# A fused linear-attention, Fourier-mixing and MLP kernel whose instruction order is a table: the table is replaced

## The chip, the cores and the metric

The kernel runs on 1 core of one Trainium2 chip. The metric is the device time of one execution in microseconds (us). The core has five engines that run side by side, each through its own list of instructions in order: TensorE (PE, matrix multiplications), VectorE (DVE), ScalarE (ACT), GpSimd (POOL) and SyncE (SP, which here only starts transfers). They wait for each other through semaphores.

## The reference

Inputs are r, k, v of shape (4, 8, 768, 48), w and u of shape (8, 48), and two MLP weights. What is computed, cut to what matters:

```python
for t in range(768):                                   # attention with a decaying state, per batch and head
    cur = einsum('bhd,bhe->bhde', u * k_t, v_t)
    y[:, :, t] = einsum('bhd,bhde->bhe', r_t, state + cur)
    state = w[None, :, :, None] * state + einsum('bhd,bhe->bhde', k_t, v_t)
x = y as (4, 768, 384)
X = fft(fft(x, axis=1), axis=2)                        # Fourier mixing, real part only
h = x + real(X)
hn = (h - mean(h)) / sqrt(var(h) + 1e-6)
out = h + relu(hn @ w_ch1) @ w_ch2                     # 384 -> 1536 -> 384
```

## The kernel before

The 768 steps of each batch are cut into 6 chunks of 128, so there are 24 chunks. Per chunk, k, r and v are loaded (192 KB each). k and r are scaled by powers of w from the tables `wtab` (the instructions with the output KR; one on DVE or POOL for each of k and r, or one on DVE for both), transposed by TensorE and copied out of PSUM (KRT), or transposed by a DMA in later chunks. Then come a score product (PSUM bank), a copy (AC) and a mask (MA) of it on ACT and POOL, or the mask straight on DVE, the u term (PR, DE, TT), the running state (S) and the output X.

A batch whose six chunks are done is folded by symmetry: HH and XF are sums and differences of halves of X, with the tensor XF as the input of the first transform (line 636 on TensorE, tables te_t and tn_t). In batch 0 this is done chunk by chunk, so the XF of its last two chunks (numbers 4 and 5) is the last input that its first transform needs. A second transform (lines 677), the residual and the statistics (UF, UB, st, MV), a transposition of the normalised rows (UNT), the first MLP product (line 765, copied out as HT) and the second (line 786, and 812 for the very last rows, added up as osb) follow for each batch. The results go out by DMA from POOL (line 799) or SP (line 800, and 822 for two half tiles at the end).

The first thing of all is the table wtab: w is loaded (line 283, the first transfer on ScalarE's queue), broadcast over the partitions by a product with a row of ones (line 322; the ones are a memset on DVE, line 286, into a part of the HT buffer), its logarithm is taken (line 324) and six exponentials are made of it (lines 326 and 328), with `icol` and `ncol` (lines 304 and 305, converted on DVE from an iota on POOL, line 288) as their factors.

No compiler orders the work. Every operation is first recorded with a number, what it reads and writes, and a list of alternatives (which engine does it, and how). `ORDER` is a table that gives the numbers in the order in which they are issued; a token such as `173.1` means operation 173 in its alternative 1. `emit` walks over it, gives each new tile the buffer of its ring that was last used longest ago, and calls the chosen alternative:

```python
for k, (n, a) in enumerate(order):
    o = self.ops[n]
    for t in o["new"]:
        ends = held[t.ring]
        m = min(range(len(ends)), key=ends.__getitem__)
...
    fn = o["alts"][a][2]
    if fn is not None:
        fn()
```

Operations 0 to 149 are matrix products of zeros (line 272) that compute nothing and may be left out; some products of zeros of 384 columns (line 366) inside the chunks are optional too. An engine's list is the subsequence of ORDER that falls to it, so the table sets each engine's order, which engine does what where there is a choice, and the buffers.

Of the kernel before, what the change touches and what calls it, by code (L numbers as in the profile page):

```python
# [95 lines left out]
152 15 159 158 28 150 160 46 151 174 155 164 8 165 173.1 196 193 202 32 34 199.1 205 203 153 208 176 181 200.1 154 182  # L96
183 184 185 187 206 209 214 215 204 207 180.1 169.1 166.1 168.1 175.1 170.1 157 178.1 172 167 274.1 156 275.1 278.2
276.1 279.2 186 310.1 211 212 201.1 378.2 189 217 271 179.1 311.1 312.1 316.1 210 280.2 213 161 315.1 281.2 188 347.1
349.1 379.2 162 163 415.3 314.1 317.1 348.1 318.1 282.2 284 351.3 353.3 319.1 283.2 352.3 287 382.1 354.3 195 198
380.2 297 333 190 191 220 218 285.1 320 216 197 221 177 384.1 385.1 321.1 286.1 194 223 301.1 277 302.1 355.3 289  # L100
383.1 386.1 288 226 303.1 337.1 452 219 304 323 313 388 222 224 296.1 453 305.1 272 227 357 322.1 324 291 325 391
306.2 513.2 387 401 339 417.3 356 420.1 389 332.1 416.3 390 358.1 359.1 338.1 350 421.1 225 423.1 6 235 419.1 392
422.1 454 362 481.1 405 360 458 482.1 307 456 459 340.1 341 424 308 364 368.1 438 381 406 342.1 457 460 363 369.1 425
426.1 361 393 428.1 429.1 442.1 427.1 461 514.2 309.1 343 1 400.1 462 465.1 370 371.1 344 346.1 372 345.1 41 418 407
430 463.1 517 443.1 466.1 273 373.1 408.1 409 444 410.1 485.2 1021 467 411.1 437.1 473 445.1 236 446 374.1 483.1 487.2
1014 486.2 488.2 455 447.1 1015 1022 412 414.1 375.1 43 546.3 515.2 464.1 519 471.1 472.1 1007 1008 489.2 491 474.1
494.1 413 377 448 376 475 484 573.2 1023 490 1009 1010 495.1 449.2 1024 450.1 1016 1017 496 476.1 477 478.2 480 479
520 1000 1001 503.1 1309 518 1002 1003 504 508.1 451 1004 1005 547.3 548.3 521 522.1 552.1 492.1 509.1 1006 1025 1026
1018 1019 493.1 510 1011 1012 551.1 1020.1 554.1 516 1013 1028 511 523 524.1 528 512 550.1 228 1027 535.1 1030 553.1
1042 1029 526 536 1058 1059.1 1308 1060.1 1061 574.2 575.2 1064 1065.1 1031 1032 1043 1078 1044 525.1 1070 1036 1037  # L110
549.2 1071 1066.1 577.2 1079.3 1072 556 557.1 579.2 542 580.2 540.1 555.1 1038 1073.2 563 567.1 559.1 1050 1033.2
578.2 1051.4 1052.4 1045.2 1055.4 1067 1081.3 581.2 569 1080.3 1039.2 1053.4 1057.4 1083.3 1085.3 560.1 1084.3 561 232
244 229 230 676.3 562 231 558.1 568.1 233 583 1082.3 586 1062.1 677.3 1371 1373 570 245 1377 234 571 680.3 584 585
639.1 1056.4 678.3 682.3 1375 582.1 1054.4 237 681.3 587 238 239 683.3 1355 572 684.3 1363 1359 1356 1374.1 1372 241
240 1378.1 686 1364 243 596 1365 1369 687 527 688 247 248 171 1360 541.1 640.1 689 690 600 576 601 606.2 608.2 543 544
1376.1 685 1366 1313 1370.1 1314 765.3 1361 588 602 595 1325 545 1074.1 1317 1318.1 1362 1075.1 1333 1334 603 607.2
1034.1 1040.1 604 1321 1331 1315 1335 1332 643.3 1327 605 1336 612.2 1322.1 609.1 641.1 621 1316 628.1 1323 645.3 1324
767.3 611.2 614.2 646.3 644.3 766.3 610.2 647.3 613.2 615 1326 1367 1368 771.4 246 250 251 1357 1310 616 617 1035.1
249 649 648 619.1 620.1 650 1311 708.1 679.2 629 635 1358 1319 1328 654 660 658.1 652.1 653.1 633.1 634.1 242 1329
1330 1320 699 691 703.1 618 636 1391 642.2 659.1 704.1 789.2 637 705 638 661 770.4 651 662 663 1063.1 192 1349 1379  # L120
709.1 769.4 706 707 1068.1 1069.1 1076.1 1343 664 1312 666 710.1 712 1350 1380 698.1 665 667 1337 1392 1344 713 668
1046.1 714 1041.1 1047.1 670 669 671 715 1338 1345 744.2 716 718 721 1351 1339 1346 1048.1 711 1352 1340 672 673 675
674 719 723 1094 1086 1087 741.2 1049 742.2 1353 730.1 1090 1091 1092 1088 756 1347 790.2 791.2 722 793.4 1095 1098
795.4 1096 1099 1100 717 1341 1089 773.4 720 794.4 1393 731 797.4 1394 1093 1097.1 735.1 772.4 775 1101 774 1104 1348
1105 1116 1381 768 1102.2 1103 757 776 1117 1106 813.3 1132 814.3 1110 1382 782 783.1 1118 745.4 815.3 1107 778 1111
1112 780 1125.4 818.4 785 1385 736.1 1119 1129.4 1113 737 738 739 1077 779 1133 784.1 792 1134 1152 1144 1386 1387
781.1 740 1136.1 1137.1 804 1138 1124 805.1 1145 1146 786 777 1135 787 743.2 1139 796.4 798.1 1395 1396 1388 817.4
1140 819.4 820.4 821.4 823 799 1141.2 1126.4 1155.4 746.4 1383 1147 1127.4 1157.4 802.1 806 809 807.1 1108.1 1354
1131.4 822.1 747.4 800.1 1128.4 1130.4 1153.4 1156.4 788 1397 801.1 1399 808.1 252 824 1398 1405 1406 825 1401 749.4
# [752 lines left out]
```

## Time and profile before

| | us |
|---|---|
| median of 3 runs | 179.48 (178.18 to 181.58) |
| profiled execution, its own time | 177.02 |
| its span, first to last instruction | 175.3 |
| TensorE busy in the span | 157.2 |
| VectorE busy | 138.7 |
| ScalarE busy | 108.4 |
| GpSimd busy | 80.8 |

The span is what the profile's times count from; 1.72 us of the profiled time lie outside it. The profiled execution was 2.46 us shorter than the median of the timed runs, and the three timed runs lie 3.4 us apart among themselves.

### The profile page before, as it was taken

To read this page: it belongs to the slowest core of one execution; us is meant where nothing else is said; L and a number is where in the kernel's file an instruction comes from. 1 tells how busy PE (TensorE), PEld (TensorE's weight loads), DVE (VectorE), ACT (ScalarE), POOL (GpSimd) and SP (SyncE) were. 2 spreads that over 40 slices of the span, in tenths; PEclk is the share of its full clock that TensorE was granted. 3 is DMA by queue.
4 is the path that set the end of the run, shared out by engine and by line. 5 is a ranking of instruction groups with operands and counts; after the bars stand their busy time and mean duration, and the time that the engine had idled before them with its cause. 6 is when DMAs were issued, how large, how long until landed. Compare 5 with 4: busy or idle time off the path is not lost. (4 is left out here: it accounts for less than half of the span.)

```text
span 175.3 us, 4260 instructions
## 1 busy us (share of the span) xinstructions
PE 157.2 (90%) x1589; PEld 111.8 (64%) x1590; DVE 138.7 (79%) x314; ACT 108.4 (62%) x260; POOL 80.8 (46%) x120
## 2 busy tenths in 40 slices
PE   6348989829999979999999899999999999999992
PEld 1136667627777756677666478667676876666661
DVE  5487999999988979999979998868899775511632
ACT  2375889528868995578996266957735770275210
POOL 6606947693776640466974453473452121020110
PEclk9999999999999999999999999999999999999999
DMA  5999989799099999999999989999500043420132
GB/s 117 219 202 212 245 166 221 181 186 175 2 184 177 203 212 201 186 238 138 213 199 230 267 174 244 187 138 227 152 0 0 4 121 81 112 95 0 45 124 100
DMA packets 98118, 27.08 MB, mean 155 GB/s; under 512 B 94369, under 2 KB 96930, under 8 KB 98098
## 3 DMA queue, kind: packets, MB, share of 16 engines
q1 hardware_dynamic: 92912, 21.70, 63.2%
q0 software_dynamic: 2064, 4.53, 11.0%
q10 hardware_dynamic: 3122, 0.59, 2.1%
q8 instruction: 12, 0.20, 0.5%
q14 instruction: 8, 0.07, 0.1%
HBM read 19.77 MB, written 4.72 MB: 140 GB/s over the span
## 5 line engine op out<-in xcount | busy, mean ns | idle before, releaser
L765 PE MATMUL bank<-UNT,W 128*128 128x384 bf16 x288 | 54.4, 326 | 0.0
L786 PE MATMUL bank<-W,HT 128*128 128x384 bf16 x276 | 51.9, 326 | 0.9 <-DMA W<-in_moe_w_ch_dram 0.9
L770 ACT ACTIVATE HT<-bank 128x384 bf16<-128x384 f32 x68 | 30.6, 494 | 27.2 <-PE bank L765 27.0
L765 PEld LDWEIGHTS <-W 128*128 128x128 bf16 x288 | 30.6, 114 | 11.5 <-DMA UNT<-UB 0.2
L786 PEld LDWEIGHTS <-HT 128*128 128x128 bf16 x276 | 25.9, 98 | 15.7 <-DMA W<-in_moe_w_ch_dram 1.1
L453 POOL TENSOR_SCALAR_AFFINE_SELECT MA<-AC 128x512 bf16<-128x512 bf16 x25 | 17.3, 701 | 10.8 <-ACT AC L451 8.4
L796 DVE SCALAR_TENSOR_TENSOR osb<-bank,rstd,UF 128x384 f32<-128x384 f32 x23 | 13.9, 614 | 9.3 <-PE bank L786 9.1
L386 POOL TENSOR_TENSOR KR<-kr,wtab 128x384 bf16<-128x384 f32 x15 | 16.5, 1106 | 7.3 <-DMA kr<-in_r_dram 5.4
L771 DVE TENSOR_SCALAR HT<-bank 128x384 bf16<-128x384 f32 x28 | 15.0, 552 | 6.1 <-PE bank L765 6.0
L386 DVE TENSOR_TENSOR KR<-kr,wtab 128x384 bf16<-128x384 f32 x29 | 16.5, 586 | 3.1 <-ACT wtab L326 2.8
L451 ACT CAST AC<-bank 128x512 bf16<-128x512 f32 x25 | 14.2, 586 | 4.1 <-PE bank L444 2.0
L799 POOL DMA_DIRECT2D out_dram<-osb x11 | 6.3, 568 | 22.0 <-DVE osb L796 19.9
L636 PE MATMUL bank<-te_t,XF 128*128 128x193 bf16 x108 | 12.2, 247 | 4.5 <-DVE XF L567 3.8
L456 DVE TENSOR_TENSOR MA<-bank,mtri 128x512 bf16<-128x512 f32 x23 | 15.4, 683 | 0.7 <-PE bank L444 0.6
L708 ACT ACTIVATE tn_t<-UF,sm 128x384 bf16<-128x384 f32 x24 | 14.8, 617 | 0.2
L410 PE MATMUL bank<-ident,KR 128*128 128x128 bf16 x112 | 12.0, 251 | 3.0 <-DVE KR L386 2.8
L432 POOL TENSOR_TENSOR PR<-KRT 128x512 bf16<-128x512 bf16 x9 | 10.4, 1156 | 7.3 <-ACT KRT L420 4.1
L636 PEld LDWEIGHTS <-XF 128*128 128x128 bf16 x120 | 9.9, 97 | 5.7 <-DVE XF L567 4.0
L689 DVE SCALAR_TENSOR_TENSOR UF<-bank,X 128x384 f32<-128x384 f32 x22 | 11.6, 548 | 1.7 <-PE bank L677 1.7
L410 PEld LDWEIGHTS <-KR 128*128 128x128 bf16 x112 | 8.8, 113 | 5.8 <-issue 3.5
L523 DVE TENSOR_TENSOR TT<-V,bank 128x384 bf16<-128x384 bf16 x19 | 10.3, 544 | 2.6 <-PE bank L514 2.5
L543 DVE TENSOR_TENSOR X<-bank,TT 128x384 bf16<-128x384 f32 x18 | 9.6, 550 | 2.4 <-PE bank L535 2.4
(108 smaller groups left out, 263.8 us busy)
## 6 DMA issues: line engine op xcount, KB each, us to landing
kr<-in_k_dram SPq DMA_DIRECT2D x23, 192.0 KB, 4.2
kr<-in_r_dram SPq DMA_DIRECT2D x23, 192.0 KB, 4.4
vt<-in_v_dram SPq DMA_DIRECT2D x23, 192.0 KB, 4.3
out_dram<-osb SPq DMA_DIRECT2D x12, 192.0 KB, 1.9
out_dram<-osb POOLq DMA_DIRECT2D x11, 192.0 KB, 3.1
W<-in_moe_w_ch_dram POOLq DMA_DIRECT2D x2, 576.0 KB, 7.5
W<-in_moe_w_ch_dram POOLq DMA_DIRECT2D x3, 384.0 KB, 6.2
te_t<-te_c SPq DMA_DIRECT2D x1, 579.0 KB, 5.4
```

What stands on the lines that cost most here:

```text
L386: eng.tensor_tensor(out=o, in0=x, in1=y, op=AluOp.mult)
L410: nc.tensor.transpose(tps[s]()[:, p, :], KR()[:, s, p, :], ident)
L451: op(("AC", i, a), [("ACT", "AC", lambda: nc.scalar.copy(AC(), A_ps[a]())), ("NONE", "", None)], r=[("A", i)], w=[("AC", i, a)], new=[AC], ...
L453: op(("MA", i, a), [("POOL", "MA", lambda: nc.gpsimd.affine_select(out=MA[a](), in_=AC(), pattern=[[0, NP], [1, 128]], base=0, channel_mul ...
L456: ("DVE", "MA", lambda: nc.vector.tensor_tensor(out=MA[a](), in0=A_ps[a](), in1=mtri.unsqueeze(1).to_broadcast([128, NP, 128]), op=AluOp.m ...
L636: nc.tensor.matmul(fp()[:, par, :], lhsT=lhsT[:, g * CH:g * CH + 128], rhs=rhs, start=(nb == 0 and par == 0), stop=(nb == last and par == ...
L708: ("ACT", "SQ", lambda: nc.scalar.activation(out=squares, in_=UF()[:, j, :], func=Act.Square, scale=-float(DM), bias=sm()[:, j:j + 1], acc ...
L765: nc.tensor.matmul(hp(), lhsT=W1[:, dt, ft // 4 * 512 + ft % 4:(ft // 4 + 1) * 512:4], rhs=UNT()[:, :, dt, :], start=(dt == 0), stop=(dt = ...
L770: op(("HT", hf, ft), [("ACT", "HT", lambda: nc.scalar.activation(out=HT()[:, ft, :], in_=hp(), func=Act.Relu, scale=-1.0)), ("DVE", "HT", ...
L771: ("DVE", "HT", lambda: nc.vector.tensor_scalar(out=HT()[:, ft, :], in0=hp(), scalar1=-1.0, scalar2=0.0, op0=AluOp.mult, op1=AluOp.max))],
L786: nc.tensor.matmul(mo(), lhsT=HT()[:, ft, j * 128:(j + 1) * 128], rhs=W2[:, ft, :], start=(ft == 0), stop=(ft == 11))
L796: one(("osb", hf, j), "DVE", "osb", lambda: nc.vector.scalar_tensor_tensor(out=osb(), in0=mo(), scalar=rstd()[:, j:j + 1], in1=UF()[:, j, ...
```

## The change

ORDER is another table. No function and no operation's definition changes; every line of code moves up by one, since the new table is one line shorter (line 386 of the profile is line 385 after the change). The diff's first lines stand for the rest:

```diff
-152 15 159 158 28 150 160 46 151 174 155 164 8 165 173.1 196 193 202 32 34 199.1 205 203 153 208 176 181 200.1 154 182
-183 184 185 187 206 209 214 215 204 207 180.1 169.1 166.1 168.1 175.1 170.1 157 178.1 172 167 274.1 156 275.1 278.2
+208 209 202 150 151 203 152 155 204 205 206 158 199.1 159 200.1 207 214 215 211 212 213 30 169 216 210 163 175 181.1
+154 160 201.1 166 167 168 164 165 170 153 182 183 184 185 274.1 275.1 172 174 156 171 178.1 276.1 188 280.1 278.1 162
...
```

Besides the order, some 230 operations change their engine, or are split or merged by their alternative. Over the whole kernel, DVE gets 5 fewer HT copies and ACT 5 more; ACT gets 6 more KRT copies and DVE 6 fewer; POOL starts 15 of the result's transfers in place of 11, and SP 10 in place of 14. The products of zeros of 512 columns go from 10 to 2, those of 384 columns from 1 to 4. Loads keep their size and number.

The start on DVE. KR, WD, XF and S are buffers that are set to zero once; the memset of `HT 1x128` is the row of ones for the first product. Before:

```order
L285 MEMSET zero 128x256
L296 MEMSET wuc 128x4
L295 MEMSET wuc 128x4
L316 MEMSET XF_100 128x6x16
L304 CAST icol<-icol_i 128x3
L305 TENSOR_SCALAR ncol<-icol 128x3
L336 MEMSET WD_82 64x4x48 x2
L286 MEMSET HT_186 1x128
L316 MEMSET XF_101 128x6x16
```

After:

```order
L284 MEMSET zero 128x256
L294 MEMSET wuc 128x4
L295 MEMSET wuc 128x4
L308 MEMSET KR_93 128x16x8
L313 MEMSET WD_83 128x384
L286 MEMSET HT_186 128x128
L308 MEMSET KR_90 128x16x8
L308 MEMSET KR_91 128x16x8
L308 MEMSET KR_92 128x16x8
L303 CAST icol<-icol_i 128x3
L304 TENSOR_SCALAR ncol<-icol 128x3
L308 MEMSET KR_94 128x16x8
L285 MEMSET HT_186 1x128
```

Four memsets of KR, one of WD and one of HT stand ahead of the cast of icol now (all of them were on POOL or stood later on DVE), and one of KR stands between ncol and the row of ones in place of two of WD.

The start on POOL, where wuc are four loads of w and u by columns. Before:

```order
L302 DMA wuc<-in_w_dram 48x4x1
L288 ISA
L288 IOTA icol_i 128x3
L315 MEMSET WD_82 128x384
L320 MEMSET S_97 128x384
L310 MEMSET KR_93 128x16x16
L310 MEMSET KR_90 128x16x16
L310 MEMSET KR_92 128x16x16
L315 MEMSET WD_83 128x384
L310 MEMSET KR_94 128x16x16
L292 AFFINE_SELECT mtri<-HT_186 128x128
```

After:

```order
L287 ISA
L287 IOTA icol_i 128x3
L301 DMA wuc<-in_u_dram 48x4x1
L319 MEMSET S_98 128x384
L301 DMA wuc<-in_w_dram 48x4x1
L288 AFFINE_SELECT ident<-HT_186 128x128
L319 MEMSET S_95 128x384
L301 DMA wuc<-in_u_dram 48x4x1
L301 DMA wuc<-in_w_dram 48x4x1
L385 TENSOR_TENSOR KR_91<-kr_103,wtab_78 128x8x48
```

The iota comes first, and the unbroken row of seven memsets is replaced by memsets and selects between four DMA issues.

The end of batch 0's fold on DVE. The last three XF are those of chunks 4 and 5. Before:

```order
L561 TENSOR_TENSOR HH0_99<-X0_142,bank2_63 128x192
L558 TENSOR_TENSOR HH0_99<-X0_142 128x192
L561 TENSOR_TENSOR HH0_99<-X0_142,bank4_65 128x192
L567 TENSOR_TENSOR XF0_100<-HH0_99 128x196
L567 TENSOR_TENSOR XF0_100<-HH0_99 128x2x98
L567 TENSOR_TENSOR XF0_100<-HH0_99 128x196
L386 TENSOR_TENSOR KR0_90<-kr2_104,wtab2_79 128x8x48
```

After:

```order
L560 TENSOR_TENSOR HH0_99<-X0_142,bank1_62 128x192
L455 TENSOR_TENSOR MA1_131<-bank4_65,mtri_70 128x512
L557 TENSOR_TENSOR HH0_99<-X0_142 128x192
L385 TENSOR_TENSOR KR1_91<-kr1_103,wtab1_78 128x8x48
L431 TENSOR_TENSOR PR3_126<-KRT3_122 128x512
L560 TENSOR_TENSOR HH0_99<-X0_142,bank3_64 128x192
L566 TENSOR_TENSOR XF0_100<-HH0_99 128x2x98
L566 TENSOR_TENSOR XF0_100<-HH0_99 128x196
L566 TENSOR_TENSOR XF0_100<-HH0_99 128x2x98
L385 TENSOR_TENSOR KR0_90<-kr0_102,wtab2_79 128x8x48
```

A mask, a KR and a PR of later chunks stand among the last HH now, ahead of the three XF.

The same place on POOL; the two DMA of W1 load the first MLP weight. Before:

```order
L567 TENSOR_TENSOR XF0_100<-HH0_99 128x2x98
L840 DMA W1_88<-in_moe_w_ch1_dram 128x3x768
L386 TENSOR_TENSOR KR0_90<-kr2_104,wtab2_79 128x8x48
L432 TENSOR_TENSOR PR3_126<-KRT3_122 128x512
L840 DMA W1_88<-in_moe_w_ch1_dram 128x3x768
L386 TENSOR_TENSOR KR2_92<-kr3_105,wtab0_77 128x8x48
L403 CAST V3_117<-vt1_109 128x384
```

After:

```order
L566 TENSOR_TENSOR XF0_100<-HH0_99 128x196
L839 DMA W1_88<-in_moe_w_ch1_dram 128x3x768
L402 CAST V1_115<-vt5_113 128x384
L839 DMA W1_88<-in_moe_w_ch1_dram 128x3x768
L385 TENSOR_TENSOR KR0_90<-kr0_102,wtab2_79 128x8x48
L452 AFFINE_SELECT MA3_133<-AC1_128 128x512
L431 TENSOR_TENSOR PR0_123<-KRT1_120 128x512
```

Between the two issues of W1 stands one cast, where a KR and a PR stood; KR, a select and PR follow.

The last transfers on SP, results (osb) and transposes of UB. Before:

```order
L747 DMA_TRANSPOSE UNT_154<-UB_179 128x9x128
L800 DMA out_dram<-osb_189 128x384 x2
L800 DMA out_dram<-osb_187 128x384
L822 DMA out_dram<-osb_190 128x192
L822 DMA out_dram<-osb_188 128x192
```

After:

```order
L746 DMA_TRANSPOSE UNT_152<-UB_180 128x9x128
L799 DMA out_dram<-osb_190 128x384
L799 DMA out_dram<-osb_188 128x384
L799 DMA out_dram<-osb_190 128x384
L821 DMA out_dram<-osb_188 128x192
```

The second half tile is gone from SP: `L821 DMA out_dram<-osb_189 128x192` is now the last row of POOL, and the last of all to be issued.

## Rows read from the trace of the kernel before

**Rows 1.** The page, part 1: busy us, share and instructions by engine.

```profile
PE 157.2 (90%) x1589; PEld 111.8 (64%) x1590; DVE 138.7 (79%) x314; ACT 108.4 (62%) x260; POOL 80.8 (46%) x120
```

**Rows 2.** Busy time by stretches: stretch, its length, engines, granted clock, DMA share, GB/s.

```profile
9.10:20.00 10.90, 8.04 (x90) 6.29 (x90) 9.38 (x23) 7.74 (x18) 5.13 (x6) 1.00 1.27 230
20.00:40.00 20.00, 14.91 (x220) 11.94 (x218) 19.80 (x41) 13.17 (x31) 14.22 (x20) 1.00 0.97 187
40.00:110.00 70.00, 68.06 (x742) 49.49 (x741) 64.56 (x148) 52.27 (x129) 38.55 (x52) 1.00 0.96 190
110.00:172.00 62.00, 61.78 (x538) 42.83 (x535) 40.10 (x91) 32.15 (x82) 16.78 (x24) 1.00 0.39 91
```

**Rows 3.** What TensorE waited for: us in total, times, longest.

```profile
PE bank L636 <- DVE XF L567: 3.8, 2, 3.1
...
PE bank L786 <- DMA W<-in_moe_w_ch_dram: 0.9, 1, 0.9
```

**Rows 4.** The timeline, start of the program: start, length, engine, what, idle before it.

```profile
1.85 0.60 ACTq L356 DMA_DIRECT2D kr<-in_r_dram  x1
...
2.45 0.44 POOL L315 MEMSET WD<- 128x384 bf16 x1
...
2.56 2.07 DVE L304 CAST icol<-icol_i 128x3 f32<-128x3 int32 x1 [1.23 <-POOL icol_i L288]
...
4.28 0.32 POOL L310 MEMSET KR<- 128x256 bf16 x1
...
5.41 0.17 DVE L286 MEMSET HT<- 1x128 f32 x1
...
5.63 1.64 PE L322 MATMUL bank<-HT 1*128 1x384 f32 x2 [1.62 <-DVE HT L286]
...
7.31 0.49 ACT L324 ACTIVATE HT<-bank 128x384 f32<-128x384 f32 x1 [4.66 <-PE bank L322]
```

**Rows 5.** DMA issues on the page: KB each, median us from issue to landing.

```profile
kr<-in_r_dram ACTq DMA_DIRECT2D x1, 192.0 KB, 5.0
...
out_dram<-osb SPq DMA_DIRECT2D x2, 96.0 KB, 1.6
```

**Rows 6.** DVE's groups from 8.4 to 38.2 us: busy, mean ns, idle before.

```profile
L386 DVE TENSOR_TENSOR KR<-kr,wtab 128x384 bf16<-128x384 f32 x12 | 7.2, 624 | 2.9 <-ACT wtab L326 2.8
...
L456 DVE TENSOR_TENSOR MA<-bank,mtri 128x512 bf16<-128x512 f32 x8 | 5.4, 682 | 0.0
L421 DVE COPY KRT<-bank 128x512 bf16<-128x512 bf16 x7 | 2.8, 416 | 0.8 <-PE bank L410 0.8
```

**Rows 7.** The timeline around the last XF, DVE, then POOL.

```profile
34.12 3.98 DVE L567 TENSOR_TENSOR XF<-HH 128x196 bf16<-128x196 bf16 x3
...
34.23 0.80 POOL L840 DMA_DIRECT2D W<-in_moe_w_ch_dram  x1
35.05 1.00 POOL L386 TENSOR_TENSOR KR<-kr,wtab 128x384 bf16<-128x384 f32 x1
36.00 1.15 POOL L432 TENSOR_TENSOR PR<-KRT 128x512 bf16<-128x512 bf16 x1
37.09 0.79 POOL L840 DMA_DIRECT2D W<-in_moe_w_ch_dram  x1
```

**Rows 8.** The XF instructions: ns least, median, most; first and last start.

```profile
L567 DVE TENSOR_TENSOR XF<-HH x7: 249/519/3180, 23.7 to 37.5; 128x196 bf16<-128x196 bf16 x7
```

**Rows 9.** TensorE's timeline: four transposes each, either side of 22.4 us.

```profile
21.70 0.63 PE L410 MATMUL bank<-ident,KR 128*128 128x128 bf16 x4 [0.22 <-POOL MA L453]
...
22.45 0.41 PE L410 MATMUL bank<-ident,KR 128*128 128x128 bf16 x4
```

**Rows 10.** The timeline at the end: the last instruction of DVE.

```profile
171.95 0.42 DVE L819 SCALAR_TENSOR_TENSOR osb<-bank,rstd,UF 128x192 f32<-128x192 f32 x1 [0.30 <-PE bank L812]
```

**Rows 11.** POOL's issues of results (line 799): ns, and us to landing.

```profile
L799 POOL DMA_DIRECT2D out_dram<-osb x11: 540/573/592, 75.5 to 168.0; - x11
...
DMA to landing us min/median/max: 2.1/3.1/3.8
```

121 rows, old and new, of the table ORDER are left out of this document.

## The prediction

> **What bounds the kernel now.** I read the page's busy times first, then the busy times by stretches, TensorE's waits, and the timeline at the three places where it waits or where the change moves something. TensorE is busy 157.2 us [rows 1], and the stretches say where it is not [rows 2]: the first 9.1 us are the start, 9.1 to 20 us lack 10.90 - 8.04 = 2.9 us, 20 to 40 us lack 5.1 us, 40 to 110 us lack 1.9 us, 110 to 172 us lack 0.2 us, and from 172 us there is only the last result's way out, 3.3 us. So from 40 us on TensorE is the bound and nearly full, and only some 2 us can be saved there. Before 40 us it is VectorE that is full (19.80 of 20.00 us) and TensorE that waits for it. The largest wait is for XF, 3.8 us in two waits, one of them 3.1 [rows 3].
>
> That wait is not work. Of VectorE's last three XF, which together take 3.98 us, one alone took 3.18, though the least of the seven is 0.249 [rows 7, 8]. In the same time GpSimd ran issue, KR, PR and issue without a gap [rows 7]. VectorE's instruction was held while GpSimd was at work. The start shows the same thing: the cast of icol, 3 columns, took 2.07 us, from 2.56 to 4.63, while GpSimd's memsets ran from 2.45 to 4.28 + 0.32 = 4.60 [rows 4]. Since the ones for the first product stand behind it on VectorE (5.41), the product (5.63), the logarithm (7.31) and all of wtab come late by that.
>
> **The change part by part.** I sum against the profiled execution's own 177.02 us.
>
> The start. VectorE is idle for 1.23 us before the cast, so it was free at 1.33 [rows 4]. In place of one small memset the new list has six ahead of the cast; five at the 0.17 of the ones' memset and WD, the widest, at GpSimd's 0.44 for as many columns give 1.3 us at most [rows 4], less the one left out: the cast is reached at about 2.5. GpSimd stands then at the end of its memset of S or in the DMA issue behind it. The best case is that the cast isn't held at all: 0.17 for each of cast, ncol, one memset and the ones end at 3.2. The worst is that it is held through GpSimd's whole unbroken list, which with two more memsets or selects of 0.44 and three issues of 0.57 to 0.80 [rows 4, 7, 11] from 2.5 on ends at 5.1 to 5.8, and the ones at 5.6 to 6.3 in place of 5.58. I take a value between, nearer the best: the last XF started at 37.5, so the long one ended about there, some 0.4 us into the second issue of W (37.09), and an issue seems to let VectorE in where a run of other work doesn't [rows 7, 8]. That gives 3.0 for the cast and 3.5 for the ones. The product also needs w, whose landing no row shows; the nearest are 1.6 us for half a tile and 5.0 us for r on the same queue [rows 5], so from 2.4 to 5.8 us. I take the product at 4.1 in place of 5.63: **-1.5 us**, bounds -2.4 and +0.7. The loads do not take this back: r of chunk 0, issued at 1.85, lands 5.0 later [rows 4, 5], at 6.9, and the scaling of r comes about 1.5 us after the logarithm, at 7.3. The third load that now stands behind it on ScalarE's queue, v of chunk 0, comes after it. Eight products of zeros that are left out, six of them at the start, cost nothing in time: TensorE has no other work there; what they may do for its clock is a rival.
>
> The chunks of batch 0, from the first KR to the last XF, where VectorE is the bound. VectorE loses two KR, three KRT copies and one mask, 2 x 0.62 + 3 x 0.42 + 0.68 = 3.2 us [rows 6]. It gains six and loses two instructions of the kinds HH, XF, PR, S, X and V, none of them cheaper when free than 0.25 [rows 8] or dearer than the mask's 0.68 [rows 6]: +1.0 to +2.7; and some seven memsets, at most 0.2 each. Together -2.2 to +0.9, and I take 0: the stage is not shorter, it starts earlier. ScalarE and GpSimd, which take what VectorE gives up, have room (13.17 and 14.22 of 20 us) [rows 2], but what GpSimd takes can hold VectorE more often.
>
> The last three XF. Before, GpSimd's issue, KR, PR and issue lasted 3.7 us [rows 7]. Now issue, cast, issue, KR and select stand there: 0.80 + about 0.5 + 0.79 + 1.00 + about 0.6 = 3.7 us, as long. But VectorE meets them with a mask, HH, KR, PR and HH first, some 2 us of work, so part of that list is over when the XF come; on the other hand HH, KR and PR have two inputs in SBUF, as XF has, and can be held as well. From -3.2 (nothing held) to +2.0 (each held in turn); I take **-0.5**. What is late next if the hold goes: the second transform and UF of batch 0, on a VectorE that has 5.4 us free between 40 and 110 [rows 2], so a gain here reaches TensorE.
>
> From 40 us on. The same matrix products in another order, at 97% and 99.6% of the time [rows 2]. The 0.9 us wait for a weight piece [rows 3] can go, since that piece is issued before two PR now; the other two pieces are issued behind these PR, where there was one in front of them before, and a late one would make TensorE wait with all second MLP products behind it. From -2.0 (no wait left) to +3.0; I take **0**.
>
> Fillers and options: TensorE does two products of zeros in place of ten, four smaller in place of one, and one residual product more. All are under half a microsecond and mostly in gaps: 0.
>
> The end. The last half tile left on SP's queue: it landed 1.6 us after its issue [rows 5]. It now leaves on GpSimd's, where whole tiles took 2.1 to 3.8 us, median 3.1 [rows 11]. Nothing hides it: it is the last thing that the program does, 171.95 + 0.42 being the end of the last sum [rows 10]. +0.5 to +2.2; a half tile is nearest to the least, so **+0.7**.
>
> Sum: -1.5 - 0.5 + 0 + 0.7 = **-1.3 us**, so 175.7 us against the profile's 177.02. The timed median stands 2.46 above it: 179.48 - 1.3 = **178.2 us**.
>
> **The rivals.** First, the start does not move: the cast is held as before, now by DMA issues as well. For it speaks the 2.07 us of the cast [rows 4] and that VectorE's long XF began at 37.5 - 3.18 = 34.3 to 34.4, during an issue, and was not done at its end [rows 7, 8]; against it, that the list has issues in it where an XF got through. The first term falls away: +0.2 us, 179.7. The Trainium skill (SBUF — State Buffer, "Who interferes with whom" and the warning above it) says that copies and casts in VectorE's two-port modes and GpSimd exclude each other for a whole instruction, and that a GpSimd DMA issue needs that port to write its descriptors. By that rule this rival holds; the trace agrees for memsets, and no row has a cast against an issue.
>
> Second, the hold goes: XF comes when GpSimd reads nothing. Then the second term is -3.2 and the sum -4.0: 175.5. For it speaks that one cast stands between the two issues where KR and PR stood; against it, that KR and PR only moved behind the second issue. The same section of the Trainium skill says that a VectorE instruction with two SBUF inputs collides only with a GpSimd one that reads SBUF, and supposes an issue to need only the write side; then issues hold nothing and this rival gains. The trace does not agree: XF began inside an issue, over half a microsecond before KR, and was held.
>
> Third, on the other side, the clock. The granted clock stands at 1.00 in all stretches [rows 2], yet four transposes took 0.63 us at 21.70 and 0.41 at 22.45 [rows 9]: TensorE's products are at its lower level (1.2 GHz) up to there, and at 2.4 after. Before that it had been busy 8.04 of 10.90 us and the products of zeros ran at the start. If the step comes later with fewer of these, say at 30 us, then of the 14.91 us that TensorE is busy from 20 to 40 us [rows 2] some 6 us would take 0.63/0.41 = 1.5 times as long, +3 us, of which TensorE's idle time there hides a little: +2.5 on the sum, +1.2 in all, so 180.7; at the far end, a step at 40 us, +5 and 183.2. It decides against us from about 27 us on. Against it: chunk work starts sooner and its products stand closer together.
>
> **How the numbers follow.** The forecast has 0.48 (own range 176.3 to 180.2), the first rival 0.17, the second 0.17, the third 0.12, and 0.06 remain for waits after 40 us that no row foretells. No change can be told from these runs within 2%, 3.6 us. Faster than 175.9: most of the second rival and the forecast's low tail, 0.22. Slower than 183.1: the third's far part, the rest, and what the timed runs scatter (3.4 us), 0.13. Within: 0.65. The range, from the second rival's lower part to the third's upper, is 174.2 to 182.4.
>
> **What would show it.** The ones' memset on VectorE at 3 to 4 us and the logarithm at about 5.8 (first rival: 5.4 and 7.3); the last XF at about 36 in place of 38.1, with one of them over 1 us (second rival: none over 0.6); four transposes at 0.4 us by 22 us (third: later than 27); TensorE lacking 2 us between 40 us and its end; and the last landing 2 us or more after its issue on GpSimd's queue. The prediction is wrong if TensorE lacks more than 5 us after 40 us, or if the time from the logarithm to the last XF, 30.8 us before, moves by more than 3.

## The result, and the profile after

The median is 174.19 us in four runs (174.01 to 174.34) against 179.21 in the runs of the kernel before beside them: ratio 0.974, interval 0.969 to 0.978, faster by 2.6%. The forecast was 178.2 with a range from 174.2, so the time lies at the very edge of the range's low end. The profiled executions differ by less: 174.01 against 177.02, spans 172.3 against 175.3, that is 3.0 us. A ratio, with its 95% interval, is taken over the runs of each program that lie within 1.5% of its fastest; on one core, as will be seen, part of the scatter that this leaves out is the program's own.

The kernel after, busy time by stretches (length, engines, granted clock, DMA share, GB/s), to be held against [rows 2]:

```profile
20.00:40.00 20.00, 15.18 (x211) 11.78 (x208) 19.10 (x43) 12.46 (x28) 11.67 (x18) 0.91 1.01 203
40.00:110.00 70.00, 69.96 (x767) 51.01 (x765) 63.15 (x144) 53.07 (x133) 43.41 (x55) 1.00 1.00 190
```

TensorE lacked 1.94 us between 40 and 110 before, and lacks 0.04 now. From 20 to 40 us its granted clock is 0.91, where it was 1.00.

The start in the timeline, against [rows 4]: VectorE, then TensorE, then ScalarE (line numbers are one lower than before).

```profile
2.25 0.10 DVE L303 CAST icol<-icol_i 128x3 f32<-128x3 int32 x1
2.40 0.49 DVE L304 TENSOR_SCALAR ncol<-icol 128x3 f32<-128x3 f32 x1
...
2.72 0.17 DVE L285 MEMSET HT<- 1x128 f32 x1
...
7.16 0.56 DVE L385 TENSOR_TENSOR KR<-kr,wtab 128x384 bf16<-128x384 f32 x1 [0.66 <-DMA kr<-in_r_dram]
...
2.97 1.64 PE L321 MATMUL bank<-HT 1*128 1x384 f32 x2 [1.10 <-DVE HT L285]
...
4.65 0.49 ACT L323 ACTIVATE HT<-bank 128x384 f32<-128x384 f32 x1 [2.00 <-PE bank L321]
```

The cast was not held at all (ncol behind it took 0.49 us, where it took 0.17 before), the ones came at 2.72 in place of 5.41, the logarithm at 4.65 in place of 7.31. Then VectorE waited for r: the next thing that is late.

The last XF of batch 0, against [rows 7], VectorE and then GpSimd:

```profile
31.88 1.77 DVE L431 TENSOR_TENSOR PR<-KRT 128x512 bf16<-128x512 bf16 x1
33.57 0.34 DVE L560 TENSOR_TENSOR HH<-X,bank 128x192 bf16<-128x192 bf16 x1
33.83 1.69 DVE L566 TENSOR_TENSOR XF<-HH 128x196 bf16<-128x196 bf16 x3
...
31.33 0.81 POOL L839 DMA_DIRECT2D W<-in_moe_w_ch_dram  x1
32.14 0.52 POOL L402 CAST V<-vt 128x384 bf16<-128x384 f32 x1
32.59 0.81 POOL L839 DMA_DIRECT2D W<-in_moe_w_ch_dram  x1
33.42 1.07 POOL L385 TENSOR_TENSOR KR<-kr,wtab 128x384 bf16<-128x384 f32 x1
34.46 0.64 POOL L452 TENSOR_SCALAR_AFFINE_SELECT MA<-AC 128x512 bf16<-128x512 bf16 x1
```

The hold is still there, but now PR pays most of it: 1.77 us, where the same form took 0.41 elsewhere. The last XF ends at 35.52, 2.58 sooner than the 34.12 + 3.98 = 38.10 of before. From the logarithm to the last XF it is 30.87 us, where it was 30.79, so in this profile the stage between them is not shorter; it starts earlier.

The end, against [rows 10, 11]: the last sum, the issue on GpSimd's queue, and the time to landing of line 821's half tiles.

```profile
167.84 0.42 DVE L818 SCALAR_TENSOR_TENSOR osb<-bank,rstd,UF 128x192 f32<-128x192 f32 x1 [0.28 <-PE bank L811]
168.56 0.54 POOL L821 DMA_DIRECT2D out_dram<-osb  x1 [0.48 <-DVE osb L818]
...
DMA to landing us min/median/max: 1.6/1.8/1.9
```

From the sum's end (168.26) to the end of the span it is 4.0 us, where it was 175.3 - 172.37 = 2.9. The last issue began 0.30 us behind the sum (0.02 before), and its landing took at most 1.9 us, where the prediction looked for 2 or more.

So the 3.0 us are: the last XF -2.58, from the last XF to TensorE's end -1.52 (132.28 in place of 133.80), and the end +1.1.

### The profile page after: what moved, and what is told of

It reads as the page before. It is cut to its first block, busy times and chain, and to the rows that moved or that the text cites. A ratio compares the mean times of both kernels' runs of the same rounds, so it can differ in the third digit from the quotient of the medians.

```text
span 172.3 us, 4247 instructions
## 1 busy us (share of the span) xinstructions
PE 155.3 (90%) x1586; PEld 111.6 (65%) x1586; DVE 136.6 (79%) x320; ACT 108.2 (63%) x258; POOL 82.0 (48%) x119
## 4 chain that ended last, share of the span: by engine, by line
PE 54%; issue 23%; DVE 11%; DMA 4%; POOL 4%; SPq 1%; POOLq 0%; ACT 0%; DVEq 0%
PE bank L764 19%; PE bank L785 14%; DMA kr<-in_r_dram 4%; PE bank L635 4%; PE bank L676 3%; PE bank L443 3%; PE bank L409 2%; DVE KR L385 2%; POOL out_dram L798 2%; PE bank L474 2%; PE bank L534 2%; PE bank L513 2%; DVE MA L455 1%; DVE XF L566 1%; DVE PR L431 1%
## 5 line engine op out<-in xcount | busy, mean ns | idle before, releaser
L769 ACT ACTIVATE HT<-bank 128x384 bf16<-128x384 f32 x73 | 33.5, 491 | 21.8 <-PE bank L764 21.6
L385 DVE TENSOR_TENSOR KR<-kr,wtab 128x384 bf16<-128x384 f32 x30 | 21.4, 727 | 3.8 <-ACT wtab L325 2.9
L798 POOL DMA_DIRECT2D out_dram<-osb x14 | 8.0, 572 | 33.9 <-DVE osb L795 33.9
L452 POOL TENSOR_SCALAR_AFFINE_SELECT MA<-AC 128x512 bf16<-128x512 bf16 x25 | 16.3, 657 | 8.7 <-ACT AC L450 8.6
L385 POOL TENSOR_TENSOR KR<-kr,wtab 128x384 bf16<-128x384 f32 x14 | 15.2, 1090 | 10.6 <-DMA kr<-in_r_dram 5.0
L795 DVE SCALAR_TENSOR_TENSOR osb<-bank,rstd,UF 128x384 f32<-128x384 f32 x23 | 13.5, 610 | 7.9 <-PE bank L785 6.8
L770 DVE TENSOR_SCALAR HT<-bank 128x384 bf16<-128x384 f32 x23 | 12.3, 548 | 6.8 <-PE bank L764 6.7
L419 ACT COPY KRT<-bank 128x512 bf16<-128x512 bf16 x20 | 11.2, 589 | 5.2 <-PE bank L409 5.0
L431 POOL TENSOR_TENSOR PR<-KRT 128x512 bf16<-128x512 bf16 x7 | 8.1, 1156 | 10.2 <-ACT KRT L419 9.7
L707 ACT ACTIVATE tn_t<-UF,sm 128x384 bf16<-128x384 f32 x21 | 12.9, 613 | 0.1
L688 DVE SCALAR_TENSOR_TENSOR UF<-bank,X 128x384 f32<-128x384 f32 x21 | 11.0, 552 | 1.6 <-PE bank L676 1.6
```

Of the source, the lines that this page charges most:

```text
L385: eng.tensor_tensor(out=o, in0=x, in1=y, op=AluOp.mult)
L452: op(("MA", i, a), [("POOL", "MA", lambda: nc.gpsimd.affine_select(out=MA[a](), in_=AC(), pattern=[[0, NP], [1, 128]], base=0, channel_mul ...
L707: ("ACT", "SQ", lambda: nc.scalar.activation(out=squares, in_=UF()[:, j, :], func=Act.Square, scale=-float(DM), bias=sm()[:, j:j + 1], acc ...
L769: op(("HT", hf, ft), [("ACT", "HT", lambda: nc.scalar.activation(out=HT()[:, ft, :], in_=hp(), func=Act.Relu, scale=-1.0)), ("DVE", "HT", ...
L770: ("DVE", "HT", lambda: nc.vector.tensor_scalar(out=HT()[:, ft, :], in0=hp(), scalar1=-1.0, scalar2=0.0, op0=AluOp.mult, op1=AluOp.max))],
L795: one(("osb", hf, j), "DVE", "osb", lambda: nc.vector.scalar_tensor_tensor(out=osb(), in0=mo(), scalar=rstd()[:, j:j + 1], in1=UF()[:, j, ...
```

## The experiments

Edits are told by the names of instructions, each line being one engine's list at the place.

**The start.** First the start alone, in the kernel before.

```diff
 VectorE, in the kernel before
-zero wuc wuc XF0 icol ncol WD WD one_f XF0 S0 one_b UW0 KR0 | KR(0)
+zero wuc wuc KR0 WD0 one_b KR0 KR0 KR0 icol ncol KR0 one_f | KR(0) UW0 XF0 ... WD XF0 WD
 GpSimd
-load(wuc) icol_i WD0 S0 KR0 KR0 KR0 WD0 KR0 mtri S0 ident S0 ... load load load
+icol_i load(wuc) S0 load ident S0 load load S0 WD0 mtri S0
```

> The kernel before, with only the memsets, selects and four small loads of the start (VectorE and GpSimd) in the order of the kernel after; every other instruction stands as it did. Theory: the start alone brings 2.7 us, one for one. Then the logarithm is at 4.6 to 4.8 us in place of 7.31, the time from it to the last XF stays at 30.8, and the profiled span is 172.6 to 173.2 in place of 175.3 (2.1 to 2.7 less; VectorE gets half a microsecond of memsets that stood in an idle stretch before). Rival: the start is only worth something with the rest of the order, since the old list of chunks waits for loads that come no sooner; then the logarithm is as early, but the time from it to the last XF grows by over 1.5 us and the span stays above 174.

The median was 177.9 against 177.7, ratio 0.996 (0.991 to 1.000): no change in the time. In the profile the ones came at 2.72 as in the kernel after, but the logarithm only at 5.61. TensorE's timeline of this run says why:

```profile
1.26 2.74 PE L272 MATMUL bank<-zero 128*128 128x512 bf16 x6 [1.26 <-DVE wuc L296]
3.93 1.64 PE L322 MATMUL bank<-HT 1*128 1x384 f32 x2
```

The six products of zeros, which the change had cut to one, run until 4.0 us and the product stands behind them. They cost nothing while the ones came at 5.4; once the ones are early they cost 3.93 - 2.97 = 1.0 us. The last XF came at 36.28, 1.82 sooner for a logarithm that was 1.70 sooner, so in the old order the start passes on one for one (30.67 us from logarithm to last XF, 30.79 before). The profiled run was 1.5 us above the median, so where it lost the gain behind 40 us (a wait of 2.1 us for V, and two falls of the clock) is not taken for the rule; that the median did not move is.

Then the hold at the start, in the kernel after.

```diff
 GpSimd, in the kernel after
-icol_i load S0 load ident S0 load load ... WD0 ... S0
+icol_i load S0 S0 WD0 S0 load ident load load
```

> The kernel after, with four memsets on GpSimd (S, S, WD, S, some 0.4 us each) put together behind its first small load, where one memset and a load stood; nothing moves on another engine. Theory: VectorE's small instruction is held as long as GpSimd works without a gap. The four memsets run from 2.3 to 3.8 us, ncol (0.49 in the kernel after, 0.17 in the kernel before) ends at about 3.9 in place of 2.89, the ones follow at 3.9, the logarithm comes at 5.7 to 5.9 in place of 4.65, and the span grows by 1.0 to 1.3. Rival: the 2.07 us that the cast of icol took before were something else, say the integers' conversion; then ncol ends by 3.0, the logarithm is at 4.65 and the span does not change.

The cast of this run, and GpSimd's list beside it:

```profile
2.25 1.58 DVE L303 CAST icol<-icol_i 128x3 f32<-128x3 int32 x1
...
2.31 0.79 POOL L319 MEMSET S<- 128x384 bf16 x2
3.02 0.44 POOL L314 MEMSET WD<- 128x384 bf16 x1
3.38 0.43 POOL L319 MEMSET S<- 128x384 bf16 x1
3.74 0.60 POOL L301 DMA_DIRECT2D wuc<-in_w_dram  x1
```

The same cast, at the same 2.25, took 1.58 us: to the end of the last memset (3.81). The logarithm came 1.39 later, at 6.04. The theory of the hold stands. Its second half fell: the last XF ended at 35.50, 0.02 sooner than in the kernel after. 0.7 of the delay went into the wait for r (the KR of 7.16 began at 7.81, with no wait), the rest into smaller holds that now met no memsets: a KR that had taken 1.34 at 13.5 us took 0.54. In this profile 1.4 us of the early start are slack. Set beside the run before it: with a late logarithm in both (5.61 and 6.04), the last XF came at 36.28 in the old order and at 35.50 in the new one, so by these two profiles 0.8 us of the gain there belong to the rest of the order and not to the start. The four runs (173.2 to 177.3) scatter too far for the time to tell more.

**The end.** One entry of the order: `1654` (GpSimd's queue) becomes `1654.1` (SP's).

> The kernel after, with the last half tile of the result on SP's queue as before, not on GpSimd's. Theory: the queue alone makes the end longer; from the last sum's end to the end of the span it is 2.9 us in place of 4.0, so the span and the time are 1.1 us shorter. Rival: the end is longer because the half tile of the other queue lands in the same moment and both share the way out; then the span changes by less than 0.4.

From the last sum's end (166.77) to the span's end (170.2) it was 3.4 us, 0.6 less than in the kernel after, 0.5 more than before. So the queue makes 0.6 of the 1.1; what makes the other 0.5 stays open. The four runs gave 173.1 in the median (171.9 to 176.1). The profiled span was 2.1 us shorter than that of the kernel after, more than the end explains, because of the next point.

**The clock.** The granted clock in this run and in the kernel after, the same stretch (37 to 38 us); TensorE's instructions up to there are the same:

```profile
37.00:38.00 1.00, 1.00 (x18) 0.93 (x17) 1.00 (x3) 0.90 (x2) 0.00 (x0) 1.00 1.15 193
```

```profile
36.00:37.00 1.00, 1.00 (x15) 0.57 (x13) 1.00 (x3) 0.60 (x1) 0.00 (x0) 0.61 1.14 192
37.00:38.00 1.00, 1.00 (x9) 0.93 (x8) 1.00 (x3) 0.17 (x1) 0.00 (x0) 0.50 1.17 199
```

The first, of the run with the end on SP's queue, stands at 1.00 (2.4 GHz) and does 18 products. The kernel after stands at 0.50 (1.2 GHz) and does 9. TensorE had waited for 1.2 and 0.9 us shortly before, in both. Neither run has a wait of TensorE behind the last XF; the one took 130.91 us from there to TensorE's end, the other 132.28: the fall costs 1.4 us, and comes in some runs and not in others. The next experiment filled the waits.

```diff
+    for m in range(24):
+        op(("idle", "fp", m), [("PE", "idle384", lambda: nc.tensor.matmul(
+            fp3().rearrange("p a m -> p (a m)"), lhsT=zero[:, 0:128], rhs=zero[:, 0:386],
+            start=False, stop=False, skip_group_check=True))], r=["zero", ("fp", 0, 3, 3)], use=[fp3])
 TensorE's order
-tp(7,1) de(6) u(6) fp(0,2,2) fp(0,2,3) fp(0,0,4)
+tp(7,1) 6 of zeros de(6) u(6) fp(0,2,2) fp(0,2,3) 5 of zeros fp(0,0,4)
```

> The kernel after, with eleven added products of zeros of 386 columns (0.16 us each at the higher level) in TensorE's two waits before the last XF of batch 0: six ahead of the bonus product that waits for PR, five ahead of the first product that waits for XF. They add zeros to a transform's sum, so nothing else changes. Theory: the granted clock fell to 0.5 from 36.2 to 39.4 us since TensorE did little from 32 to 36; with the waits filled it stays at 1.00 and the span is 1.3 to 1.8 us shorter. Rival 1: the fall has another cause (the work on all engines at once); then it comes all the same, the span is the same or 0.3 longer. Rival 2: TensorE has slack there; then the clock stays at 1.00 and the span is less than 0.5 shorter.

The clock stayed at 1.00 from 35 to 40 us, as the theory had it, and the time was not shorter (175.1, runs of 174.8 to 175.9; profiled span 173.0). TensorE now waited 1.9 us behind 40 us, 1.4 of them for UF near 76 us. These had not been there in the kernel after.

**The same kernel again.**

> The kernel after, unchanged, in more runs beside the kernel before on the same chip. Theory: its time has two sources of scatter that the traces so far show, a fall of the granted clock near 36 us (mean clock 0.99 or less, 1.6 to 2 us) and the KR of 73.3 us, which VectorE finished in 1.17 us in the kernel after and in 3.08 us in the run with the four memsets, though it began within 0.02 us of the same time. Then the runs scatter over some 4 us, those with a mean clock of 0.997 or more are the fastest (near 172), and the ratio to the kernel before is 0.97 to 0.985. Rival: these two belong to the changed kernels alone; then all runs lie within 0.5 us of 174.2 as in the first measurement.

Six runs gave 173.2 to 175.8, median 174.17, beside 23 of the kernel before at 177.96 (176.3 to 181.8): ratio 0.981 (0.976 to 0.986), an interval that reaches to either side of a gain of 2%. The scatter is 2.5 us, less than expected, and all six had a mean clock of 0.990 or less: none was free of the fall. But the profiled run of the same program now shows a wait that the first one did not have. VectorE's three KR there, the UF behind them, and GpSimd's list:

```profile
71.81 5.12 DVE L385 TENSOR_TENSOR KR<-kr,wtab 128x384 bf16<-128x384 f32 x3
76.85 0.55 DVE L688 SCALAR_TENSOR_TENSOR UF<-bank,X 128x384 f32<-128x384 f32 x1
...
71.45 1.17 POOL L431 TENSOR_TENSOR PR<-KRT 128x512 bf16<-128x512 bf16 x1
72.67 1.06 POOL L654 COPY TR<-TT 97x768 bf16<-97x768 bf16 x1
73.68 0.59 POOL L798 DMA_DIRECT2D out_dram<-osb  x1
74.27 0.86 POOL L402 CAST V<-vt 128x384 bf16<-128x384 f32 x1
```

And what TensorE waited for behind it in that run:

```profile
PE bank L676 <- DVE UF L688: 1.3, 1, 1.3
PE bank L785 <- DVE UF L688: 0.5, 1, 0.5
```

In the first profile of the kernel after, the same place, VectorE and GpSimd:

```profile
72.17 2.80 DVE L385 TENSOR_TENSOR KR<-kr,wtab 128x384 bf16<-128x384 f32 x3
74.89 0.54 DVE L688 SCALAR_TENSOR_TENSOR UF<-bank,X 128x384 f32<-128x384 f32 x1
...
74.04 0.59 POOL L798 DMA_DIRECT2D out_dram<-osb  x1
74.76 0.58 POOL L402 CAST V<-vt 128x384 bf16<-128x384 f32 x1
```

There GpSimd had a gap of 0.13 us ahead of V (74.63 to 74.76), here it had none (73.68 + 0.59 = 74.27), and the KR were held for 3.65 us in all in place of 1.3. In the runs with the four memsets and with the filled waits it was 3.7 and 3.3 us. The gap is not what decides, though. In the run with the end on SP's queue V followed its issue without a gap (72.35 + 0.59 = 72.94), and the three KR were held for 1.1 us only:

```profile
70.73 2.55 DVE L385 TENSOR_TENSOR KR<-kr,wtab 128x384 bf16<-128x384 f32 x3
...
72.35 0.59 POOL L798 DMA_DIRECT2D out_dram<-osb  x1
72.94 0.71 POOL L402 CAST V<-vt 128x384 bf16<-128x384 f32 x1
```

What lets a KR in at one place of the list and not at another stays open. TensorE has some stock of work there; what goes beyond it becomes its wait.

**Clearing GpSimd's list at the last XF.** In the kernel after, and in the kernel before:

```diff
 GpSimd, in the kernel after
-XF load(W1) V(6) load(W1) KR(8) MA(6)
+XF load(W1) load(W1) MA(6)
 VectorE: PR(6) HH XF XF XF KR(8) KR(9), and behind them now KR(8); V(6) goes to ScalarE
```

> The kernel after, with GpSimd's list cleared while VectorE does PR, HH and the last three XF of batch 0: the conversion of V of chunk 6 goes to ScalarE, KR of chunk 8 to VectorE behind the XF, and the two loads of W1 stand one behind the other. Theory: the data instructions of GpSimd held PR (1.77 us, least 0.41) and two XF (0.79 and 0.68, least 0.25); without them the last XF ends 1.8 to 2.3 us sooner, at 33.2 to 33.7 us, TensorE's two waits of 1.2 and 0.9 us shrink below 0.5 each, and the span is 1 to 2.3 us shorter (VectorE has one KR of 0.55 more behind). Rival: the issues of the two loads hold VectorE as well; then PR, which meets the first of them at 31.9, still takes 1.1 us or more, and the last XF ends no more than 1 us sooner.

```diff
 GpSimd, in the kernel before
-XF load(W1) KR(8) PR(7) load(W1) KR(9) V(8)
+XF load(W1) load(W1) KR(9) V(8)
 VectorE: XF XF XF, and behind them now KR(8), and PR(7) behind TT(6)
```

> The kernel before, with KR of chunk 8 and PR of chunk 7 taken from GpSimd and put on VectorE behind the last XF of batch 0, and the two loads of W1 one behind the other. Theory: the XF that took 3.18 us was held by KR and PR; without them it takes 0.3 to 0.9 us, the last XF ends at 35 to 36 us in place of 38.10, TensorE's wait of 3.13 us falls below 1.2, and the span is 1.5 to 2.5 us shorter. Rival 1: an issue alone holds it; then it lasts to the end of the second issue, 35.8 us, or longer, and the gain at the last XF is under 2 us. Rival 2: the gain is there at the last XF but is lost behind it, as in the run with the new start, to a fall of the granted clock or to a wait for a load; then the span is less than 1 us shorter.

The timeline of the first of the two, VectorE and GpSimd:

```profile
32.62 0.41 DVE L431 TENSOR_TENSOR PR<-KRT 128x512 bf16<-128x512 bf16 x1
32.95 0.34 DVE L560 TENSOR_TENSOR HH<-X,bank 128x192 bf16<-128x192 bf16 x1
33.22 1.22 DVE L566 TENSOR_TENSOR XF<-HH 128x196 bf16<-128x196 bf16 x3
...
32.06 1.59 POOL L839 DMA_DIRECT2D W<-in_moe_w_ch_dram  x2
33.66 0.65 POOL L452 TENSOR_SCALAR_AFFINE_SELECT MA<-AC 128x512 bf16<-128x512 bf16 x1
```

And of the second:

```profile
33.24 1.89 DVE L567 TENSOR_TENSOR XF<-HH 128x196 bf16<-128x196 bf16 x3
...
33.35 1.55 POOL L840 DMA_DIRECT2D W<-in_moe_w_ch_dram  x2
34.93 1.05 POOL L386 TENSOR_TENSOR KR<-kr,wtab 128x384 bf16<-128x384 f32 x1
```

PR, inside the issues, took 0.41 in place of 1.77, and XF in the second run 1.89 for three in place of 3.98 (one of them 1.08, with nothing but two issues beside it). So it is GpSimd's data instructions that hold for long; an issue alone cost 0 in the one run and 0.8 in the other. The last XF ended at 34.44 (1.1 sooner; 0.8 had been lost to a new hold of HH at 23 us) and 35.12 (3.0 sooner, 0.7 of them from an earlier logarithm). In time the second gave 176.1 against 178.0, ratio 0.994 (0.990 to 0.997), clear of no change but under 2%. The first scattered from 172.1 to 178.9 in ten runs, with a median of 176.6, which is no gain over the 174.2 of the kernel after; its ratio of 0.976 (0.970 to 0.982) to the kernel before rests on three of the ten. In its profile one KR near 72 us was held for 4.8 us and TensorE waited 3.2.

**Clearing it at 72 us.** The first attempt combined three edits: the end on SP's queue, the filled waits, and V of chunk 14 on ScalarE.

> The kernel after with three edits together: the last half tile on SP's queue, the eleven products of zeros in the two waits before 36 us, and the conversion of V of chunk 14 on ScalarE in place of GpSimd, so that GpSimd has a gap behind its load issue at 74 us and the KR that VectorE begins at 73.3 is let in there. Theory: the edits remove the clock's fall (1.6 us), the hold of 1.9 us and 0.6 us at the end; all runs lie at 171.5 to 172.5 us, and the mean clock is 0.995 or more. Rival: the hold at 73 us has another cause than the unbroken list behind the issue; then that KR takes 2.5 us or more in the profile and the time stays above 173.5.

It missed: 175.3 (174.8 to 177.0), and a KR of 1.97 us. TensorE also waited 0.8 us for a V from ScalarE. With V gone from GpSimd's list, TT moved up to its place, 0.03 us behind the issue, so there was no gap; the edit did not make what it was to test. The next one took the work away on the other side of the issue.

```diff
 GpSimd, in the kernel after
-store(out) PR(15) TR(1,1) store(out) V(14) TT(13) MA(13)
+store(out) store(out) V(14) TT(13) MA(13)
 VectorE
-TT2 KR(16) KR(16) KR(14) UF UF UF
+TT2 KR(16) PR(15) TR(1,1) KR(16) KR(14) UF UF UF
 and 1654 becomes 1654.1
```

> The kernel after with the last half tile on SP's queue, and with GpSimd's list cleared at the place where three KR of VectorE (72 to 76 us) were held by 1.3 us in one run of the same instructions and by 3.7, 4.8 and 3.2 in others: PR of chunk 15 and the reversed copy TR of batch 1 go from GpSimd to VectorE (0.41 and 0.36 us there), among the KR. Theory: these holds are what makes TensorE wait near 77 us in some runs (1.8 to 3.2 us) and not in others; then no KR between 71 and 76 us takes over 0.8 us, TensorE has no wait over 0.3 us between 70 and 80, the end is 0.6 us shorter, and the times scatter less: 171.5 to 173.5, the rest of the scatter being the clock's fall at 36 us. Rival: the waits near 77 us come from late loads or from the second transform itself; then they come again in part of the runs, and the times reach 175 us as in the kernel after.

VectorE's list in its profile, and GpSimd's V:

```profile
72.07 0.54 DVE L385 TENSOR_TENSOR KR<-kr,wtab 128x384 bf16<-128x384 f32 x1
72.53 0.42 DVE L431 TENSOR_TENSOR PR<-KRT 128x512 bf16<-128x512 bf16 x1
72.89 0.36 DVE L654 COPY TR<-TT 97x768 bf16<-97x768 bf16 x1
73.17 1.02 DVE L385 TENSOR_TENSOR KR<-kr,wtab 128x384 bf16<-128x384 f32 x2
74.11 0.55 DVE L688 SCALAR_TENSOR_TENSOR UF<-bank,X 128x384 f32<-128x384 f32 x1
...
73.08 1.47 POOL L402 CAST V<-vt 128x384 bf16<-128x384 f32 x1 [0.85 <-DMA vt<-in_v_dram]
```

VectorE has two instructions more, and comes to UF 0.8 us sooner than in the better profile of the kernel after. No KR was held, GpSimd itself stood idle for 0.85 us (its V waited for a load), TensorE did not wait there, and all six runs lie from 171.6 to 173.5: median 172.5, ratio 0.969 (0.964 to 0.974) to the kernel before beside it (177.85). This version beats both kernels: its dearest run is below every one of the ten runs of the kernel after but one, and its interval lies below that of the kernel after's repeat. How much of that is the clearing is not shown by the times: the end on SP's queue alone had given 173.1 in four runs, ratio 0.972 (0.964 to 0.980), though one of the four took 176.1. The profile says what the clearing is worth: from the last XF to TensorE's end it takes 132.29 us, as in the kernel after's first profile, where the KR cost TensorE nothing, and 2.1 us less than in its second (134.43). So it saves the bad case only.

**With the waits filled as well, and with both places cleared.** The edits are those shown above, put together.

> As the run before, and with the eleven products of zeros in TensorE's two waits before 36 us. Theory: the granted clock doesn't fall at 36 us, so the span is another 1.3 to 2 us shorter than in those runs of e9 whose mean clock is 0.99 or less, some 170 to 171.5 us in all, with a mean clock of 0.995 or more in most runs. Rival: the fall only moves to another place (in the run with three edits together it stood at 17 to 21 us) and costs as much there; then the mean clock is 0.99 or less in half the runs and the times are those of e9.

The median was 173.0 (172.1 to 173.7). The profiled clock did not fall, yet the span, 171.4, is that of the run without the products (171.6), since the last XF came 0.3 later and TensorE waited 0.8 us at 66 and 113 us. The two runs with a mean clock of 1.00 took 173.1 and 173.3, no less than those at 0.99. The theory of the gain fell: the fall costs TensorE 1.4 us in a trace, but in this profile filling the waits cost as much elsewhere.

> The two clearances together: the kernel of e9 (the list of GpSimd cleared at 72 us, the last half tile on SP's queue) and the edits of e6 (cleared at 32 us as well). Theory: the last XF comes 1 to 2 us sooner than in e9, at 33.7 to 34.4 us, but the loads are not sooner: in e6 VectorE's KR of 64.7 us waited 1.4 us for its r, and TensorE 1.1 us behind it. So the gain at 34 us is given back to that wait, and the median lies within 0.8 us of the 172.5 of e9. Rival: the wait for r in e6 was chance; then the gain of 1 to 2 us stays and the median is 170.5 to 171.5.

The median was 172.5, as forecast (171.8 to 172.7, and one run of 175.7: with both places cleared a long run still came). The profile had the last XF at 33.81, 1.6 sooner than without the second edit, and a wait of TensorE of 1.1 us at 59 us for a mask, with a KR held for 1.2 ahead of that mask on VectorE; VectorE waited for r only 0.3 us. So the gain is given back, but the reason I gave was not what this profile shows.

**The load of W2.**

```diff
 GpSimd, in the kernel before
-MA(7) MA(12) MA(12) TT(9) KR(10) KR(15) load(W2) load(W2)
+load(W2) MA(7) MA(12) MA(12) TT(9) KR(10) KR(15) load(W2)
```

> The kernel before with the first third of W2 loaded some 6 us earlier (ahead of a select of chunk 7 on GpSimd); nothing else moves. Theory: of the 2 us that TensorE lacked after 40 us before and not after, 0.9 were this load; then TensorE's wait at 63.5 us is gone, its other waits stay, and the span is 0.9 us shorter for the same start. Rival: the loads share the way in, so that another one comes late in its place; then a new wait of 0.5 us or more stands between 50 and 70 us, or in the first transform of batch 1, and the gain is under 0.4.

The rival was right: the wait for the weight is gone and others, at 59 to 60 and 84 to 86 us among them, add up to 2.5 us in place of 2.1. The median is 177.6 against 177.9, ratio 0.998 (0.995 to 1.001).

## Why the prediction was right, and where its sizes were off

The direction was right, but the forecast had given only 0.22 to a change faster by more than 2%, and that the time lies within the range is partly luck: its low end was set for the second rival, whose mechanism did not come (two XF took 0.79 and 0.68, where it wanted none over 0.6, and PR took 1.77). The first rival (the start does not move) and the third (the clock's step comes later) fell at the places named: the logarithm at 4.65, and eight transposes in 0.73 us at 18.91, so TensorE is at its upper rate by 19 us, not later than [rows 9] but earlier:

```profile
18.91 0.73 PE L409 MATMUL bank<-ident,KR 128*128 128x128 bf16 x8
```

The forecast was 4.0 us too long. 2.3 of them are no term: I carried the 2.46 us between the median and the profile of before over to the kernel after, whose median is 0.2 above its profile. In the 66 runs of the kernel before that stand beside the experiments the medians are 177.6 to 178.0, so 0.6 to 0.9 above the profile; the first four runs (178.2 to 181.6) had been higher, for a reason that no run shows, and the gain is nearer 3.5 us than 5.0 (0.981 in the repeat). The other 1.7 are terms:

The start, -1.5, was mis-sized: the logarithm came 2.66 sooner, beyond the bound of 2.4. The cast, whose end I had put at 3.0, was reached at 2.25 and not held, and the product did not wait for w, which I had put between 2.4 and 5.8: it began at 2.97, behind the ones. "Eight products of zeros cost nothing" held for the old start only; leaving out five of them is 1.0 of the 2.66, as the first experiment showed. What I missed behind it is that the wait for r then takes 0.7 of it back. At the last XF I had -2.0 in all, and it is -2.58.

The last three XF, -0.5, was right in size: the holds of PR and XF there add up to 1.36 + 0.54 + 0.44 = 2.3 us over the least of their forms, where one XF had paid 2.9. That HH, KR and PR can be held as XF is came true for PR.

From 40 us on I had 0, with -2.0 if no wait was left. The first profile has the -2.0, less 1.4 for a fall of the clock that I did not foresee, and 0.9 more that stays open. It is not less work: the trace has 1300 products behind the last XF, where it had 1298. The step that failed is what I thought decided it: the place of the weights' loads. Moving a load in the kernel before gave nothing; what came and went in the kernel after is the hold of three KR at 72 us, 1.3 us or 3 to 5. So the term was -1.5 in the first profile (132.28 from the last XF to TensorE's end, in place of 133.80) and +0.6 in the second (134.43). What both profiles share is the last XF, 2.58 and 2.95 us sooner. Which part of the change the gain in the median comes from is not shown: the start alone brought the last XF 1.82 us sooner and left the median where it was, and with the start made late again in the kernel after the last XF came no later.

The end, +0.7, is +1.1, with 0.6 for the queue; a landing of 2 us or more, which I had named as its sign, did not come (at most 1.9). The second rival's mechanism, tried alone in the old order, took 2.3 us from the last XF (3.0 less the earlier start) and left 1 to 2 in the time.

Of the Trainium skill's rule (SBUF — State Buffer, "Who interferes with whom") that a VectorE instruction with two SBUF inputs collides only with a GpSimd one that reads SBUF, and of its inference that an issue needs only the write side: PR at 0.41 inside two issues agrees, the XF of 1.08 us beside two issues does not. Its other rule, that a cast in a two-port mode and a GpSimd that has to write descriptors exclude each other, is hardly tried here: the cast of 0.10 us began at 2.25, 0.06 us before the issue beside it ended (1.54 + 0.77 = 2.31), so it met only the issue's last piece.

## What to carry to other kernels

Where VectorE and GpSimd are both busy, read GpSimd's list beside every VectorE instruction that takes more than its least time: a held instruction can pay for as much as the whole unbroken list, and taking work off GpSimd there can make VectorE faster though it does that work itself (two instructions more at 72 us, and 0.8 us sooner through). A hold that goes in a profile need not come back as time: 3.0 us at the last XF left 1 to 2. One profile of such a program is one sample; take a second before a wait is called gone. When a start is made early, ask what stood there for free: products of zeros, a load.

## What the runs showed of the hardware

A cast of 3 columns that starts at 2.25 us took 0.10, 0.60 or 1.58 us (kernel after, end on SP's queue, four memsets). GpSimd's next memset began 0.05 to 0.06 us behind it in all three. The hold goes both ways: GpSimd's conversion of V took 1.47 us beside three VectorE instructions (0.52 elsewhere). TensorE's granted clock went to 0.50 near 36 us, behind 2 to 3 us of waits, in five profiles, and did not in the kernel before behind a wait of 3.1 us (with the new start alone it did, behind the same wait), nor in the run whose end is on SP's queue behind the same waits as in the kernel after. What decides it is open. The recorded clock of a program's start is to be read with the products beside it. In the kernel before with the cleared list it is 0.50 from 8 to 21 us, in the kernel before itself 1.00 [rows 2], and yet four transposes take the same in both, here

```profile
20.14 0.61 PE L410 MATMUL bank<-ident,KR 128*128 128x128 bf16 x4
```

and there 0.63 us at 21.70 [rows 9]: TensorE was at its lower level in both. The difference stands earlier. The two products of the start, at 5.63 in both, took 0.91 us with the cleared list and 1.64 without [rows 4], which is where the 0.7 us of its earlier logarithm come from. So a mean clock of 0.96 there beside 1.00 is no sign of a slower run.
